# The second half of a down tile one pair later in its group of eight pairs

## The chip, the cores and the metric

The kernel runs on 1 core of one Trainium2 chip. The metric is the device time in microseconds of one execution: 1829.32 us in the median of 3 runs (1829.18 to 1830.04).

## The reference

One transformer block, prompt phase, in float32: adaptive layer norm, full attention with 32 heads of 16, and a SwiGLU feed-forward network. S = 2048 rows, D = 512, F = 1792.

```python
mod = (_silu(c) @ w_mod).reshape(c.shape[0], 6, 1, -1)      # sa, ca, ga, sb, cb, gb
h = _layernorm(x) * (1 + ca) + sa
q, k, v = split(h @ wqkv)                                    # 32 heads of 16
p = softmax(q @ k.T * 16 ** -0.5)
x = x + ga * ((p @ v) @ wo)
h = _layernorm(x) * (1 + cb) + sb
x = x + gb * ((_silu(h @ w_gate) * (h @ w_up)) @ w_down)
```

## The kernel before, in words

A float32 product is made of three products of rounded parts: every large operand is held as a high and a low part, and high x high, high x low and low x high are added up in one PSUM bank. For the scores the parts of a head stand below each other, so that one matmul over 48 or 50 rows does all of it.

**Pairs.** Attention is cut into units, one for each of four column chunks of 512 queries and each of eight groups of four heads, and each unit into 16 steps of 128 keys. One step has four **pairs** (`pair_of`, lines 977 to 989). A pair is one score matmul (`score`, line 563: keys x queries of one head into a bank, and behind it, on ACT, the exp of line 571 which reads that bank and writes a tile `pt_`) and one matmul for the row maxima of a later unit (`max_one`, line 512, with the reduce of line 523 on DVE). The two stand in opposite halves of the 128 rows, so TensorE runs them side by side. Pairs with an even head put the score first, the others the maximum. The maxima run ahead of the scores by LEAD steps, so in the last 80 pairs there are none.

**PV.** `pv_step` (line 573) multiplies the exps with the values, half a step at a time, four matmuls side by side; it follows the scores at a distance (line 1017).

**Filler.** Beside attention the feed-forward network of the chunk before is worked off: the jobs of line 695 in a list, `gate_up` (line 842) and `down` (line 866). A job is a generator (`accumulate`, line 776) which issues one step of two matmuls for each `take`. The matmuls are again over half the rows each: in the first half of the job the tile `outs[0]` is fed from rows 0 to 63 and `outs[1]` from rows 64 to 127 side by side, in the second half they trade rows. A gate/up job has 48 steps; it is spread over two groups. A down job has 12 steps, 6 for each half, and lies in one group. The two tiles are banks 3 and 6 (FBANKS).

**The trade of a down tile.** Before the second half of a down job may add into the banks from the other rows, `read_both` (line 891) has ACT copy one element of each bank (line 893); the second half's matmuls wait for these copies. A gate/up job has no such copies. Behind the last step of a down job DVE adds both banks to the residual rows (line 870), and with t0 = 2 the load of the next down weights is issued on SP's queue (line 880).

**Groups.** `filled` (line 1056) issues one group: eight pairs, and behind pair r as many steps of the job as `places[r]` says; then what `hook` holds back, then six PV half-steps, then `turns_behind`. Calls that are due at a step come behind pairs 3 and 7. In a group the scores use banks 4 and 5 in turn and the maxima banks 0, 1 and 2 (line 1060). Once the maxima are over, the row of places is looked up in `ALONE` and the scores have five banks (line 1062). Groups of gate/up take the row `TWO` twice, each down job takes the row `DOWN` once (line 1103). A down job comes with t0 = 0 and right behind it with t0 = 2. Between the parts of the network there are stretches of pairs without filler (`plain`, line 1041). The order on each engine is the order in which this program issues the instructions.

Of the kernel before, what the change touches and what calls it, by code (L numbers as in the profile page):

```python
# [47 lines left out]
NORM = 9  # L48
STARTS = (147, 275, 403)
TWO = (0, 3, 2, 2, 2, 2, 1, 0)  # L50
DOWN = (0, 3, 3, 0, 3, 3, 0, 0)
ALONE = {TWO: (0, 4, 0, 4, 0, 4, 0, 0), DOWN: (0, 6, 0, 0, 0, 6, 0, 0)}


# [47 lines left out]
def block_kernel(ctx, tc, x, wqkv, wo, w_gate, w_up, w_down, c, w_mod, out):  # L102
# [953 lines left out]
    def filled(places, work):  # L1056

        nonlocal four, bank, beside
        beside = True
        four, bank = three, Turn(4, 5)  # L1060
        if done >= 4 * n - 4 * (LEAD - 1):
            places, bank = ALONE.get(places, places), Turn(4, 5, 0, 1, 2)
        for r in range(len(places)):
            pair_of()
            take(work, places[r])
            if r % 4 == 3:
                end_steps()
        hook()
        pvs(6, False)
        turns_behind()  # L1070
# [14 lines left out]
    for ci in range(last):  # L1085
# [12 lines left out]
        for _ in range(len(ch.jobs) - (KEEP if ci == last - 1 else 0)):  # L1098
# [3 lines left out]
            work = job(ch, *args, outs, True)  # L1102
            for places in (TWO, TWO) if job is gate_up else (DOWN,):
                filled(places, work)
# [80 lines left out]
```

## Time and profile before

| | |
|---|---|
| median of 3 runs | 1829.32 us (1829.18 to 1830.04) |
| span of the profiled execution, first to last instruction | 1827.6 us |
| granted TensorE clock, mean | 1.000 |
| down tiles beside attention | 38 |

The profile gives a span for the profiled execution and no time of its own beside it; the 1.7 us between the span and the median of the runs lie before the first and behind the last instruction. PE stands for TensorE's matmuls and PEld for its weight loads, DVE for VectorE, ACT for ScalarE, POOL for GpSimd, SP for SyncE, whose queue issues DMAs. L569 is line 569 of the kernel. In a timeline row stand the start and the duration in us, engine, line, operation, tiles written and read, and in brackets how long the engine sat idle before it and what ended that. A duration of several merged instructions (x6) reaches from the first start to the last end. A matmul's duration is longer than its slot: the next matmul starts before its end.

### The profile page before, as it was taken

To read this page: it belongs to the slowest core of one execution; us is meant where nothing else is said; L and a number is where in the kernel's file an instruction comes from. 1 tells how busy PE (TensorE), PEld (TensorE's weight loads), DVE (VectorE), ACT (ScalarE), POOL (GpSimd) and SP (SyncE) were. 2 spreads that over 40 slices of the span, in tenths; PEclk is the share of its full clock that TensorE was granted. 3 is DMA by queue.
4 is the path that set the end of the run, shared out by engine and by line. 5 is a ranking of instruction groups with operands and counts; after the bars stand their busy time and mean duration, and the time that the engine had idled before them with its cause. 6 is when DMAs were issued, how large, how long until landed. Compare 5 with 4: busy or idle time off the path is not lost.

```text
span 1827.6 us, 41072 instructions
## 1 busy us (share of the span) xinstructions
PE 1818.3 (99%) x16904; PEld 1199.7 (66%) x16904; DVE 1523.2 (83%) x2554; ACT 1255.7 (69%) x2434; POOL 459.9 (25%) x538
## 2 busy tenths in 40 slices
PE   9999999999999999999999999999999999999999
PEld 7876444444455777776565777776464577767887
DVE  5578999999999888889999888889999988821544
ACT  4223888888888776777888777777888877774211
POOL 3612544556223111111123111111113011130200
PEclk9999999999999999999999999999999999999999
DMA  9884876667845454453544554444643536333742
GB/s 306 288 225 143 202 195 178 178 167 200 206 81 125 103 123 142 114 148 71 144 110 107 139 125 119 124 115 91 160 79 57 119 89 162 130 119 120 276 167 110
DMA packets 80488, 267.63 MB, mean 146 GB/s; under 512 B 19604, under 2 KB 24212, under 8 KB 59620
## 3 DMA queue, kind: packets, MB, share of 16 engines
q1 hardware_dynamic: 61324, 179.71, 34.1%
q0 software_dynamic: 18288, 84.49, 19.4%
q8 instruction: 133, 2.18, 0.5%
q10 hardware_dynamic: 688, 0.80, 0.2%
q14 instruction: 55, 0.45, 0.1%
HBM read 201.85 MB, written 62.13 MB: 144 GB/s over the span
## 4 chain that ended last, share of the span: by engine, by line
PE 82%; DVE 14%; ACT 1%; DMA 1%; issue 0%; SPq 0%; DVEq 0%; ACTq 0%
PE bank L584 21%; PE bank L786 20%; PE bank L569 14%; DVE mx L523 14%; PE bank L521 11%; PE bank L211 7%; PE bank L796 7%; DMA wm_ab<-in_w_mod 1%; PE bank L770 0%; DMA kop<-o_dr 0%; PE bank L163 0%; DMA rb<-d_dr 0%; ACT sq L820 0%; PE bank L839 0%; DVE v_flat L870 0%
## 5 line engine op out<-in xcount | busy, mean ns | idle before, releaser
L523 DVE TENSOR_REDUCE mx<-bank 128x1 f32<-128x512 f32 x2048 | 1274.3, 686 | 108.3 <-PE bank L521 54.6
L569 PE MATMUL bank<-qop,kop 50*128 50x512 f32 x2048 | 728.6, 425 | 0.4 <-ACT pt__16523 L571 0.2
L521 PE MATMUL bank<-kop,qop 48*128 48x512 f32 x2048 | 725.1, 425 | 0.3
L569 PEld LDWEIGHTS bank<-qop,kop 50*128 50x128 f32 x2048 | 343.6, 184 | 167.9 <-issue 49.7
L521 PEld LDWEIGHTS bank<-kop,qop 48*128 48x128 f32 x2048 | 344.0, 185 | 107.0 <-DVE mx L523 62.3
L786 PE MATMUL bank<-act,wgu 64*128 64x512 f32 x1872 | 301.4, 392 | 0.0
L786 PEld LDWEIGHTS bank<-act,wgu 64*128 64x128 f32 x1872 | 197.1, 187 | 24.3
L611 POOL TENSOR_TENSOR on<-o,rb 128x512 f32<-128x512 f32 x31 | 39.8, 1285 | 506.3 <-DMA rb<-d_dr 358.9
L786 PE MATMUL bank<-wd,mid 64*128 64x512 f32 x912 | 134.1, 397 | 0.1
L858 POOL CAST mid<-m 128x512 fp32r<-128x512 f32 x40 | 24.3, 607 | 380.9 <-DVE m L856 180.2
L786 PEld LDWEIGHTS bank<-wd,mid 64*128 64x128 f32 x912 | 88.3, 186 | 15.5 <-ACT first L893 3.2
L211 PE MATMUL bank<-hT,wqs 128*128 128x512 f32 x384 | 94.4, 397 | 0.4 <-DVE wqs L351 0.4
L854 DVE SCALAR_TENSOR_TENSOR q<-th,bank 128x512 f32<-128x512 f32 x56 | 38.2, 683 | 54.3 <-ACT th L850 54.3
L211 PEld LDWEIGHTS bank<-hT,wqs 128*128 128x128 f32 x384 | 70.7, 188 | 18.8 <-issue 2.9
L850 ACT ACTIVATE th<-bank 128x512 f32<-128x512 f32 x56 | 33.3, 594 | 57.9 <-PE bank L796 57.9
L870 DVE TENSOR_TENSOR x<-bank,x 128x512 f32<-128x512 f32 x84 | 53.9, 685 | 19.0 <-PE bank L786 16.8
L856 DVE TENSOR_TENSOR m<-bank,q 128x512 f32<-128x512 f32 x56 | 38.7, 692 | 21.7 <-PE bank L796 19.7
L859 POOL TENSOR_TENSOR mid<-m,mid 128x512 fp32r<-128x512 f32 x40 | 51.6, 1289 | 3.3
L796 PE MATMUL bank<-wd,mid 128*128 128x512 f32 x216 | 51.5, 394 | 0.0
L211 PE MATMUL bank<-wqs,hT 128*128 128x512 f32 x192 | 48.1, 398 | 0.0
L786 PE MATMUL bank<-wgu,act 64*128 64x512 f32 x288 | 47.0, 393 | 0.0
L796 PEld LDWEIGHTS bank<-wd,mid 128*128 128x128 f32 x216 | 40.4, 188 | 9.0 <-POOL mid L859 0.2
(6301 smaller groups left out, 5148.9 us busy)
## 6 DMA issues: line engine op xcount, KB each, us to landing
wgu<-gu_dr SPq DMA_DIRECT2D x48, 1024.0 KB
wd<-wd_dr SPq DMA_DIRECT2D x28, 1024.0 KB
kop<-kd SPq DMA_DIRECT2D x33, 768.0 KB
kop<-kd POOLq DMA_DIRECT2D x29, 768.0 KB, 8.7
gu_dr<-wgu POOLq DMA_DIRECT2D x14, 1024.0 KB, 13.6
kd<-prt SPq DMA_DIRECT2D x16, 512.0 KB
qd<-prt SPq DMA_DIRECT2D x16, 512.0 KB
kop<-gu_dr SPq DMA_DIRECT2D x8, 1024.0 KB
```

The source lines that it names most:

```text
L211: nc.tensor.matmul(pt, lhs(a, k), rhs(b, k), start=(n == 0), stop=(n == 3 * nk - 1))
L521: nc.tensor.matmul(pm, qop[u][rows, s, qt * P:(qt + 1) * P], kop[u % 3][rows, s, kc * CW:(kc + 1) * CW], start=True, stop=True)
L523: nc.vector.tensor_reduce(mx[u][:, b, s, qt, kc:kc + 1], pm, op=ALU.max, axis=AX.X)
L569: nc.tensor.matmul(sp, kop[u % 3][rows, h // 2, kt * P:(kt + 1) * P], qop[u][rows, h // 2, :], start=True, stop=True)
L584: nc.tensor.matmul(pv[u][32 * h:32 * h + 32, cols], v_flat[:, e0:e0 + 32], p_[h][:, cols], start=(kt == 0 and half == 0), stop=(kt == 15), ...
L611: mul.tensor_mul(on, o, rb)
L786: nc.tensor.matmul(outs[e], lhs(e, a, k)[rows], rhs(b, k)[rows], start=(ph == 0 and j == 0), stop=(j == z and (ph == 1 or trade is not None)),
L796: nc.tensor.matmul(outs[e], lhs(e, a, k), rhs(b, k), start=(j == 0), stop=(j == z))
L854: nc.vector.scalar_tensor_tensor(q, th, 1.0, outs[0], op0=ALU.add, op1=ALU.mult)
L856: nc.vector.tensor_mul(m32, outs[1], q)
L859: (nc.gpsimd if slow else nc.vector).tensor_sub(mid[:, 1, :], m32, mid[:, 0, :].bitcast(F32))
L870: nc.vector.tensor_add(ch.x2[:, t, :], outs[e], ch.x2[:, t, :])
```

## The change

The row of places of a down job that lies beside attention is another one. The six steps of the first half stay behind pairs 1 and 2 (pairs are counted from 0); the six of the second half stand behind pairs 5 and 6, not 4 and 5. Between the halves, and so between the copies of line 893 and the matmuls that wait for them, stand pairs 3, 4 and 5, where there were 3 and 4; behind the tile stands pair 7, where there were 6 and 7. `DOWN` as a key of `ALONE` changes with it, its row there stays.

```diff
 TWO = (0, 3, 2, 2, 2, 2, 1, 0)
-DOWN = (0, 3, 3, 0, 3, 3, 0, 0)
+DOWN = (0, 3, 3, 0, 0, 3, 3, 0)
 ALONE = {TWO: (0, 4, 0, 4, 0, 4, 0, 0), DOWN: (0, 6, 0, 0, 0, 6, 0, 0)}
```

## The prediction

> **What bounds the kernel now.** I read the page first, for the chain that ended last, and then the waits of the edited place.
>
> ```profile
> span 1827.6 us, 41072 instructions
> PE 1818.3 (99%) x16904; PEld 1199.7 (66%) x16904; DVE 1523.2 (83%) x2554; ACT 1255.7 (69%) x2434; POOL 459.9 (25%) x538
> PE 82%; DVE 14%; ACT 1%; DMA 1%; issue 0%; SPq 0%; DVEq 0%; ACTq 0%
> ```
>
> PE carries 82% of the chain and DVE 14%. The span is 1827.6 us and the median of the runs 1829.32, so 1.7 us lie around the span; I work in the span and add the 1.7.
>
> Next come the down tile's own rows. The first fence is line 893 (the tiny copies that read both banks between the halves), the second line 870 (the two adds that close a tile) up to the time at which the last row maximum of line 523 is over.
>
> ```profile
> L893 ACT COPY first<-bank x76: 143/148/150, 630.6 to 1658.5; 1x1 f32<-1x1 f32 x76
> who waited for it (us, times):
>   PEld bank L786: 3.2, 16
> ```
> ```profile
> L870 DVE TENSOR_TENSOR x<-bank,x x68: 678/687/693, 632.8 to 1588.2; 128x512 f32<-128x512 f32 x68
> ```
>
> Two copies and two adds belong to each tile. So 76/2 = 38 down tiles stand beside attention, and 68/2 = 34 of them while row maxima still run; the other 4 take the row that the table ALONE gives for them, which the diff leaves as it is. All that PE waits for the copies is 3.2 us in 16 waits. This 3.2 us bounds what covering the trade better can win directly.
>
> The third view is the table of stretches. The first sum is over the 17 groups of tiles with t0 = 0, each from its first pair to the next group's first pair, the second over the 17 with t0 = 2. The last two rows are one gate/up group with the same 8 pairs, 12 filler steps and 6 PV steps, and the longest down group.
>
> ```profile
> sum 116.25, PE 116.25 PEld 83.25 DVE 108.66 ACT 79.91 POOL 39.88; mean PE 6.84 PEld 4.90 DVE 6.39 ACT 4.70 POOL 2.35
> ...
> sum 117.81, PE 117.69 PEld 82.66 DVE 109.12 ACT 81.67 POOL 8.09; mean PE 6.92 PEld 4.86 DVE 6.42 ACT 4.80 POOL 0.48
> ...
> 641.90:648.65 6.75, 6.75 (x78) 4.95 (x74) 5.55 (x10) 4.56 (x8) 0.00 (x0) 1.00 0.68 279
> ...
> 716.47:723.67 7.20, 7.08 (x76) 4.80 (x73) 6.58 (x13) 4.63 (x10) 0.00 (x0) 1.00 0.14 20
> ```
>
> A down group takes 6.84 or 6.93 us, against 6.75 for the same slots in a gate/up group. The present place of the second half thus costs 0.09 to 0.18 us a group, 116.25 + 117.81 - 34 x 6.75 = 4.6 us in all. DVE is busy for 6.4 of the 6.9 us, ACT for 4.7: PE is the bound, DVE is close behind.
>
> The last view is the timeline of the first group (t0 = 0), and of the places in the second (t0 = 2) where it differs. I count the pairs of a group from 0.
>
> ```profile
> 628.18 0.18 PEld L569 LDWEIGHTS bank<-qop,kop 50*128 50x128 f32 x1 [0.41 <-issue]
> 628.74 0.87 PE L786 MATMUL bank<-wd,mid 64*128 64x512 f32 x6
> 629.43 0.39 PE L521 MATMUL bank<-kop,qop 48*128 48x512 f32 x1
> 629.45 0.41 PE L569 MATMUL bank<-qop,kop 50*128 50x512 f32 x1
> 629.67 0.89 PE L786 MATMUL bank<-wd,mid 64*128 64x512 f32 x6
> 629.90 0.60 ACT L571 ACTIVATE pt__7336<-bank 128x512 f32<-128x512 f32 x1
> 630.37 0.39 PE L521 MATMUL bank<-kop,qop 48*128 48x512 f32 x1
> 630.40 0.64 PE L569 MATMUL bank<-qop,kop 50*128 50x512 f32 x2
> 630.55 0.18 PEld L569 LDWEIGHTS bank<-qop,kop 50*128 50x128 f32 x1 [0.19 <-ACT pt__7336 L571]
> 630.55 0.18 PEld L521 LDWEIGHTS bank<-kop,qop 48*128 48x128 f32 x1
> 630.56 0.20 ACT L893 COPY first<-bank 1x1 f32<-1x1 f32 x2
> 630.63 0.42 PE L521 MATMUL bank<-kop,qop 48*128 48x512 f32 x1
> 630.83 0.60 ACT L571 ACTIVATE pt__7349<-bank 128x512 f32<-128x512 f32 x1
> 630.88 0.90 PE L786 MATMUL bank<-wd,mid 64*128 64x512 f32 x6
> 631.32 0.59 ACT L571 ACTIVATE pt__7352<-bank 128x512 f32<-128x512 f32 x1
> 631.62 0.39 PE L569 MATMUL bank<-qop,kop 50*128 50x512 f32 x1
> 631.85 0.86 PE L786 MATMUL bank<-wd,mid 64*128 64x512 f32 x6
> 632.82 1.29 DVE L870 TENSOR_TENSOR x<-bank,x 128x512 f32<-128x512 f32 x2
> 633.12 0.11 PEld L584 LDWEIGHTS bank<-pt__7263,v_flat 128*32 128x32 f32 x1 [0.24 <-issue]
> 634.02 1.28 DVE L523 TENSOR_REDUCE mx<-bank 128x1 f32<-128x512 f32 x2
> 634.98 0.18 PEld L569 LDWEIGHTS bank<-qop,kop 50*128 50x128 f32 x1 [0.41 <-issue]
> ...
> 637.64 0.60 ACT L571 ACTIVATE pt__7433<-bank 128x512 f32<-128x512 f32 x1
> 637.71 0.54 PEld L786 LDWEIGHTS bank<-wd,mid 64*128 64x128 f32 x6 [0.16 <-ACT first L893]
> 640.03 0.11 PEld L584 LDWEIGHTS bank<-pt__7352,v_flat 128*32 128x32 f32 x1 [0.25 <-issue]
> ```
>
> Pair 2 is at 629.43, then the three steps that end the first half, pair 3 at 630.37, pair 4 at about 630.6, the second half from 630.88, pair 5 inside it at 631.62, the rest of it from 631.85, pairs 6 and 7, and PV from 633.12. A slot of PE (a pair, or a step of two matmuls) is about 0.23 us: 631.62 to 631.85. What matters most is the row at 630.55. The scores have two banks in turn, 4 and 5, so pair 4 needs the bank that the exp of pair 2 (pt__7336) reads until 630.50; its weight load starts 0.05 us later, its matmuls at 630.63. From score to free bank a bank is thus away for 630.55 - 629.45 = 1.1 us. Two pairs in a row with three steps ahead of them just fit into that, since PE comes to pair 4 at 630.37 + 0.23 = 630.60 anyhow.
>
> **The change part by part.** 34 groups change. The number of instructions on PE, ACT, DVE and every queue stays; only places move.
>
> The copies. They stand behind pair 2 as before and PE now comes to the second half a pair later. They are done by 630.56 + 0.20 = 630.76, so the waits on them end in the 34 groups. That is the gain aimed at, at most 0.18 us in a group.
>
> The third pair. Pair 5 now follows pair 4 directly. It takes the bank of pair 3, whose exp (pt__7349) stands behind the copies on ACT, starts at 630.83 and ends at 631.43. PE is ready for pair 5 at 630.63 + 0.23 = 630.86. With the release that pair 4 shows (630.50 to 630.63, of which I take 0.11) pair 5 starts at 631.54: PE stands for 0.68 us. Behind the waiting score in PE's queue stand the maximum of pair 5 and all twelve matmuls of the second half; behind those wait DVE's adds and the maxima, and nobody else's work fills the hole. The second half then starts 0.25 us later, at 631.79 (630.63 to 630.88 is that step after the held pair 4). From there to PV stood 633.12 - 630.88 = 2.24 us with three pairs in it; one pair fewer makes 2.01. PV starts at 633.80, 0.68 us later than before.
>
> For t0 = 2 the same sum starts from the exp at 637.64: it ends at 638.24, pair 5 starts at 638.35, the second half at 638.60, PV at 640.61 against 640.03, so 0.58 us later. Here the wait on the copies and its aftermath (the 0.09 us by which these groups are longer) is what is won.
>
> A rule of matmul order bears on this. Both weight loads at 630.55 start together, the one of the maximum in the other half of the rows too: nothing passed the held score there. The Trainium skill, "TensorE: Matmul & The Clock Gate", Part 3, says that matmuls start and end in program order while weight loads may be pulled ahead of running ones; by the first half of it the hold reaches all that follows, by the second the restart would be hidden, 0.02 us less a group or 0.7 us in all (no row here shows a load passing a held one).
>
> The adds. They come after the maximum of pair 6 instead of pair 5. The second half runs from 631.79 over three steps to pair 6 at 632.48 and over three more from 632.71; the adds started 0.97 us behind the first of the last three (631.85 to 632.82), so now at 633.68, 0.86 us later, and end at 634.97 after their 1.29. The next group starts at 634.98 + 0.68 = 635.66, and its first step into banks 3 and 6 comes behind its pair 1, 0.56 us on (628.18 to 628.74 in this group), at 636.22: 1.25 us to spare, cost nothing. The cover is that spare time; beyond it each us of delay counts in full.
>
> The DMAs. The load of the next down weights is issued behind the last step with t0 = 2, about 0.9 us later, and the gate/up load behind it on SP's queue moves with it. In the emitted order nothing on SP or POOL changes places, since a group's other calls come behind pairs 3 and 7. The gate/up load of 640.05 is read one group pair later, two times 6.75 us, and the wait table shows no wait of PE for it; I take nothing.
>
> ```profile
> 640.05 0.42 SPq L715 DMA_DIRECT2D wgu<-gu_dr  x1
> ```
>
> Sum: 17 x 0.68 + 17 x 0.58 = 21.4 us. Bounds: if pair 5 starts as the exp ends and the restart is one bare slot, t0 = 2 gives 638.24 + 0.23 + 2.01 - 640.03 = 0.45 us, and 34 x 0.45 = 15.3; if every held restart drags as the second half after 637.71 does (0.09 more), 0.77 x 34 = 26.2. Nothing below zero comes out unless pair 5 is not held at all, which is a rival.
>
> **The rivals.** Forecast: held third pair, 1827.6 + 21.4 + 1.7 = 1850.7 us, range 1844.6 to 1855.5.
>
> Not held: pair 5 finds its bank free when PE comes, since ACT has slack (4.7 of 6.9 us busy). Then the groups come down to the 6.75 of the gate/up group, -4.6 us, 1824.7. It decides at the exp of pair 3: that would have to end by 630.75 and not at 631.43. For it speaks only ACT's mean load; against it, that its score starts no earlier than 630.37 and none of the exps shown takes under 0.59. Were it that matmuls behind the held score pass it, the time would be about the same, 1824.7.
>
> DVE falls behind: reduces and adds, 6.4 us in a group of 7.5, come in a clump after the hold and the adds end over 1.25 us late, so that the next tile waits. The worst group on the page, 7.20 against 6.93, gives a price of 0.3: 10 us more, 1860.9. Against it: the hold gives DVE more time, not more work.
>
> That the diff would not act where it should is no case: the key of ALONE is the same name as the row.
>
> **How the numbers follow.** Held 0.86, not held 0.08, DVE behind 0.06. A measurement of this kernel tells about 0.2%, 3.7 us, from no change. Held and DVE behind are slower, 0.92; not held is split between the full 4.6 us and less, faster 0.04 and same 0.04. The range 1844 to 1856 is that of the held case and leaves out 0.14.
>
> **What would show it.** In the changed profile: the weight load of pair 5's score idle about 0.7 us in each of the 34 groups, ended by the exp of pair 3; down groups of 7.5 us for both t0, gate/up groups still 6.75; waits on line 893 down to the four tiles without maxima; the adds behind three reduces and no wait of line 786 on them. Wrong would be a third score that starts before that exp's end, or groups longer than 7.6 us, which would point to DVE.

## The result and the profile after

The changed kernel takes 1848.87 us (1848.37 to 1850.34) against 1829.25 us before: 19.6 us more, a ratio of 1.011 with a 95% interval of 1.0097 to 1.0123. The span of its profiled execution is 1846.7 us, 19.1 more than before.

First the page of the changed kernel: span, and the chain by engine.

```profile
span 1846.7 us, 41083 instructions
PE 82%; DVE 14%; ACT 3%; issue 1%; DMA 0%; SPq 0%; DVEq 0%; ACTq 0%
```

PE's share stays at 82%, ACT's goes from 1% to 3%: at some places the chain now runs over ACT. The table of stretches says where the time is. The first sum is over the 17 groups with t0 = 0, the second over those with t0 = 2, and the last row is the gate/up group that follows the first two.

```profile
sum 127.47, PE 120.40 PEld 81.03 DVE 116.07 ACT 81.73 POOL 39.67; mean PE 7.08 PEld 4.77 DVE 6.83 ACT 4.81 POOL 2.33
...
sum 127.57, PE 120.10 PEld 80.26 DVE 110.75 ACT 83.52 POOL 7.84; mean PE 7.06 PEld 4.72 DVE 6.51 ACT 4.91 POOL 0.46
...
642.11:648.86 6.75, 6.75 (x76) 5.02 (x72) 5.22 (x9) 4.57 (x8) 0.00 (x0) 1.00 0.69 285
```

Both kinds of down group now take 7.50 us, 127.47 - 116.25 = 11.2 and 127.57 - 117.81 = 9.8 us more, 21.0 in all; the gate/up group keeps its 6.75. (A gate/up job has 24 steps, 12 in each of its two groups, not 48: `TWO` adds up to 12.) PE's busy time is on average 0.42 us short of the stretch in a group with t0 = 0 (127.47 - 120.40 over 17), where it filled the stretch before. The hole is seen in the timeline of the first group.

```profile
627.16 0.18 PEld L569 LDWEIGHTS bank<-qop,kop 50*128 50x128 f32 x1 [0.41 <-issue]
...
629.35 0.39 PE L521 MATMUL bank<-kop,qop 48*128 48x512 f32 x1
629.39 0.63 PE L569 MATMUL bank<-qop,kop 50*128 50x512 f32 x2
629.53 0.18 PEld L569 LDWEIGHTS bank<-qop,kop 50*128 50x128 f32 x1 [0.18 <-ACT pt__7336 L571]
629.55 0.20 ACT L893 COPY first<-bank 1x1 f32<-1x1 f32 x2
629.63 0.41 PE L521 MATMUL bank<-kop,qop 48*128 48x512 f32 x1
629.83 0.60 ACT L571 ACTIVATE pt__7349<-bank 128x512 f32<-128x512 f32 x1
630.32 0.59 ACT L571 ACTIVATE pt__7352<-bank 128x512 f32<-128x512 f32 x1
630.47 0.18 PEld L569 LDWEIGHTS bank<-qop,kop 50*128 50x128 f32 x1 [0.76 <-ACT pt__7349 L571]
630.47 0.50 PE L569 MATMUL bank<-qop,kop 50*128 50x512 f32 x1 [0.44 <-ACT pt__7349 L571]
630.81 0.87 PE L786 MATMUL bank<-wd,mid 64*128 64x512 f32 x6
631.95 0.69 DVE L523 TENSOR_REDUCE mx<-bank 128x1 f32<-128x512 f32 x1 [0.21 <-PE bank L521]
632.73 1.29 DVE L870 TENSOR_TENSOR x<-bank,x 128x512 f32<-128x512 f32 x2
632.77 0.11 PEld L584 LDWEIGHTS bank<-pt__7263,v_flat 128*32 128x32 f32 x1 [0.37 <-issue]
633.93 0.68 DVE L523 TENSOR_REDUCE mx<-bank 128x1 f32<-128x512 f32 x1
634.64 0.18 PEld L569 LDWEIGHTS bank<-qop,kop 50*128 50x128 f32 x1 [0.41 <-issue]
```

Up to 629.63, pair 4, this is the group of before, 1.0 us earlier. Then pair 5's score waits for pt__7349, the exp of pair 3, which ends at 629.83 + 0.60 = 630.43, and starts at 630.47. I call such a wait a hold. Two numbers in these rows tell of it and neither is its length. The weight loads sat idle for 0.76 us, but PE was still at work for part of it. The matmuls sat idle for 0.44, but that counts only from the end of the matmul before, whose tail normally overlaps the next. The length is the start against the start without a hold: 630.47 - (629.63 + 0.23) = 0.61 us. The other down groups show the same: without a hold pair 5's score would start 0.23 us behind pair 4's, and in the 34 groups it starts 0.88 to 0.94 us behind it, once 1.07.

The second view is line 893 of the changed kernel.

```profile
who waited for it (us, times):
  PEld bank L786: 1.1, 4
```

From 16 waits and 3.2 us, 4 waits and 1.1 us are left, those of the four tiles without maxima. The change does what it says: the trade is covered in all 34 groups. What covers it is longer than the wait was.

### The profile page after: what moved, and what is told of

It reads as the page before. It is cut to its first block, busy times and chain, and to the rows that moved or that the text cites. A ratio compares the mean times of both kernels' runs of the same rounds, so it can differ in the third digit from the quotient of the medians.

```text
span 1846.7 us, 41083 instructions
## 1 busy us (share of the span) xinstructions
PE 1823.2 (99%) x16904; PEld 1192.9 (65%) x16904; DVE 1525.5 (83%) x2554; ACT 1259.3 (68%) x2434; POOL 459.7 (25%) x538
## 3 DMA queue, kind: packets, MB, share of 16 engines
q0 software_dynamic: 18288, 84.49, 19.1%
## 4 chain that ended last, share of the span: by engine, by line
PE 82%; DVE 14%; ACT 3%; issue 1%; DMA 0%; SPq 0%; DVEq 0%; ACTq 0%
PE bank L584 21%; PE bank L786 19%; PE bank L569 14%; DVE mx L523 14%; PE bank L521 10%; PE bank L796 8%; PE bank L211 7%; PE bank L839 1%; PE bank L770 0%; DMA wm_ab<-in_w_mod 0%; PE bank L163 0%; ACT sq L820 0%; DVE v_flat L870 0%; PE bank L535 0%; ACT first L893 0%
## 5 line engine op out<-in xcount | busy, mean ns | idle before, releaser
L569 PE MATMUL bank<-qop,kop 50*128 50x512 f32 x2048 | 736.3, 427 | 14.9 <-ACT pt__8512 L571 0.6
L521 PE MATMUL bank<-kop,qop 48*128 48x512 f32 x2048 | 733.3, 426 | 0.3
```

Source lines behind the costliest of these rows:

```text
L521: nc.tensor.matmul(pm, qop[u][rows, s, qt * P:(qt + 1) * P], kop[u % 3][rows, s, kc * CW:(kc + 1) * CW], start=True, stop=True)
L569: nc.tensor.matmul(sp, kop[u % 3][rows, h // 2, kt * P:(kt + 1) * P], qop[u][rows, h // 2, :], start=True, stop=True)
```

## The experiments

My theory is the round trip: a score bank is away for about 1.1 us from its score to the end of its exp, there are two, and so the third score in a row waits. The rivals are that the two copies ahead of the exp on ACT cause the delay, that DVE's pace does (6.4 us of work in the group), and that the later place of the second half costs by itself. For each kernel the fence shows the sum over its 34 down groups from the table of stretches (before: 234.06, or 6.88 a group; changed: 255.04, or 7.50), and, where the verdict rests on them, rows of the timeline. The first four ran beside the kernel before at 1829.34 us.

**Four pairs in a row.**

```diff
-DOWN = (0, 3, 3, 0, 0, 3, 3, 0)
+DOWN = (0, 3, 3, 0, 0, 0, 3, 3)
```

> The second half behind pairs 6 and 7, four pairs in a row before it. Round trip (my theory: the third score in a row waits until the exp of two pairs earlier has left its bank): pair 5 is held until 3.3 us from the group's first pair as in the changed kernel, pair 6 in turn until the exp of pair 4 ends, about 3.8; the second half starts at 4.1, a group takes 7.73 us and the kernel 1857 us. Rival, copies: the two copies ahead of the exp of pair 3 cause the hold once; a further pair adds nothing, 7.50 us and 1849. Rival, DVE: the maxima of the pairs in a row run out of their three banks and DVE's 0.65 us a reduce is the pace; four pairs add one reduce, 8.1 us and 1870.

```profile
sum 263.51, PE 248.99 PEld 164.60 DVE 223.20 ACT 161.58 POOL 47.00; mean PE 7.32 PEld 4.84 DVE 6.56 ACT 4.75 POOL 1.38
```
```profile
630.49 0.18 PEld L569 LDWEIGHTS bank<-qop,kop 50*128 50x128 f32 x1 [0.76 <-ACT pt__7349 L571]
630.98 0.18 PEld L569 LDWEIGHTS bank<-qop,kop 50*128 50x128 f32 x1 [0.19 <-ACT pt__7352 L571]
```

1856.73 us, 7.75 us a group. The fourth score waits in its turn for the exp of pair 4, 0.49 us behind the third, which is the distance of two exps on ACT (629.83 and 630.32 above). That speaks for the round trip; DVE's 8.1 us a group and the copies' single hold are out as the pace here.

**One step between pairs 4 and 5, and two.**

```diff
-DOWN = (0, 3, 3, 0, 0, 3, 3, 0)
+DOWN = (0, 3, 3, 0, 1, 2, 3, 0)
```
```diff
-DOWN = (0, 3, 3, 0, 0, 3, 3, 0)
+DOWN = (0, 3, 3, 0, 2, 1, 3, 0)
```

> One step of the second half behind pair 4, two behind pair 5, three behind pair 6. Round trip: pair 5 still starts at 3.3 us, but 0.25 us of the hold is filled with the step; group 7.25 us, kernel 1840.5 us. Rival, copies: the step waits for the copies, and nothing of the hold is filled, 7.50 and 1849. Rival, DVE: the pace of three reduces is the same, 7.50 and 1849.

> Two steps of the second half behind pair 4, one behind pair 5, three behind pair 6. Round trip: pair 5 comes due at 3.17 us and is held until 3.3; group 6.98 us, 0.1 above the kernel before, kernel 1832 us. Rival, place: if each slot by which the second half starts later has its own price, one step in three is left, 7.09 us and 1835. Rivals copies and DVE: as for one step, 7.50 and 1849.

```profile
sum 246.90, PE 242.64 PEld 161.05 DVE 225.13 ACT 165.22 POOL 47.54; mean PE 7.14 PEld 4.74 DVE 6.62 ACT 4.86 POOL 1.40
```
```profile
630.37 0.18 PEld L569 LDWEIGHTS bank<-qop,kop 50*128 50x128 f32 x1 [0.48 <-ACT pt__7349 L571]
```
```profile
sum 239.47, PE 239.34 PEld 161.24 DVE 220.85 ACT 162.02 POOL 47.21; mean PE 7.04 PEld 4.74 DVE 6.50 ACT 4.77 POOL 1.39
```
```profile
631.00 0.18 PEld L569 LDWEIGHTS bank<-qop,kop 50*128 50x128 f32 x1 [0.36 <-ACT pt__7349 L571]
```

1840.43 us and 7.26 a group with one step, 1833.25 us (ratio 1.0018, interval 1.0009 to 1.0028) and 7.04 with two. So the price goes 7.50, 7.26, 7.04, 6.88 with none, one, two and three steps between. The copies and DVE, by which nothing would be won, are out as causes of the whole. But the steps are nearly even, and 7.04 lies midway between the 6.98 of the round trip and the 7.09 of the place (the rival by which the later place costs by itself): the times of these two runs don't tell those theories apart. The rows speak for the round trip. In both runs pair 5 still waits for the exp of pair 3 and starts 3.30 us into its group (the groups start at 627.07 and 627.70), and with two steps it was due at 3.18.

**A spare bank.** The score of pair 5 in down groups takes a bank of the maxima's ring; the maximum of pair 5 is held over and issued ahead of pair 6. `lone` is true at pair 5 of a down group, and `r` is the number of the maximum. A bank that is handed to `score` is used in place of the one in turn.

```diff
...
+        r = done + 4 * (LEAD - 1)
         work = [lambda: score(i + 1, h)]
-        if done < most:
-            work.insert(1 - h % 2, lambda: max_one(done + 4 * (LEAD - 1)))
+        if lone and done < most:
+            held.append(r)
+            spare = four("spare")
+            work = [lambda: score(i + 1, h, spare)]
+        elif done < most:
+            work.insert(1 - h % 2, lambda: max_one(r))
+            if held:
+                work.insert(0, lambda: max_one(held.pop()))
...
```

> The changed kernel, but the score of pair 5 in down groups goes to a bank of the maxima's ring, which the maximum of pair 2 has left by then; the maximum of pair 5 is issued with pair 6, so a group has one slot of PE more. Round trip: no hold at pair 5, which starts at 2.65 us; group 6.75 + 0.23 = 6.98 us, kernel 1831.5 us. Rival, copies: the bank does not matter, 7.5 to 7.7 us, 1849 to 1857. Rival, DVE: the same reduces in the same order, 7.5 us and 1849.

```profile
sum 247.09, PE 243.56 PEld 166.46 DVE 225.00 ACT 161.76 POOL 47.64; mean PE 7.16 PEld 4.90 DVE 6.62 ACT 4.76 POOL 1.40
```
```profile
629.41 0.41 PE L521 MATMUL bank<-kop,qop 48*128 48x512 f32 x1
629.66 0.39 PE L569 MATMUL bank<-qop,kop 50*128 50x512 f32 x1
629.67 1.09 PE L786 MATMUL bank<-wd,mid 64*128 64x512 f32 x6
630.41 1.01 PE L521 MATMUL bank<-kop,qop 48*128 48x512 f32 x2
630.92 0.18 PEld L521 LDWEIGHTS bank<-kop,qop 48*128 48x128 f32 x1 [0.42 <-DVE mx L523]
```

1841.96 us, 7.27 a group: less than half of the gain that I expected (7.50 to 6.98). The hold at pair 5 is gone (its score starts 0.25 us behind pair 4, at 629.66, and the second half beside it). In its place the maximum of pair 6 waits for a reduce, since the ring of three banks had lent one. The weight loads sit idle for 0.42 us there; the maximum itself starts 0.28 us late, at 630.92 and not at 630.41 + 0.23. My number missed this wait, and the slot more that I had counted is not there.

The next three ran beside the kernel before at 1828.74 us.

**The same, without the spare bank.** The control moves the maximum in the same way, but the score of pair 5 takes its bank in turn.

```diff
             held.append(r)
             spare = four("spare")
-            work = [lambda: score(i + 1, h, spare)]
+            work = [lambda: score(i + 1, h, None)]
```

> The counterpart of the run with the spare bank: the maximum of pair 5 is issued with pair 6 as there and the maxima's ring skips a bank as there, but the score of pair 5 takes its bank in turn, that of pair 3. Round trip: pair 5 is held until 3.3 us again, the hold at pair 6 goes since DVE has had time; group 7.4 to 7.5 us, kernel 1846 to 1849 us. Rival, DVE: what was won with the spare bank came from moving the maximum, so it is won here too, 7.2 us or less and 1842 or less.

```profile
sum 255.60, PE 241.00 PEld 162.15 DVE 218.67 ACT 165.33 POOL 47.08; mean PE 7.09 PEld 4.77 DVE 6.43 ACT 4.86 POOL 1.38
```
```profile
629.81 0.18 PEld L569 LDWEIGHTS bank<-qop,kop 50*128 50x128 f32 x1 [0.73 <-ACT pt__7349 L571]
```

1849.96 us, 7.52 a group, and the old hold for the exp of pair 3. Place, copies and the moved maximum are the same in these two kernels. What differs is the bank of pair 5's score, and with it which of banks 4 and 5 the later scores take: it is the bank. This settles what the times with one and two steps left open; the place of the second half has no price of its own that these runs show.

**The copies behind the exp of pair 3.** `read_both` is called behind pair 3 instead of with the last step of the first half.

```diff
-                          halves and read_both)
+                          halves and (lambda: trades.append(read_both)))
...
             pair_of()
+            if r == 3:
+                while trades:
+                    trades.pop()()
```

> The changed kernel with the two copies of the trade issued behind pair 3, so on ACT behind the exp of pair 3 instead of ahead of it. Round trip: that exp starts 0.45 us after its score with or without the copies, 2.66 us from the group's first pair; pair 5 still starts at 3.3, group 7.5 us, kernel 1849 us. Rival, copies: the 0.2 us of the copies stand in the exp's way; pair 5 starts at 3.1, group 7.3, kernel 1842 us.

```profile
sum 254.62, PE 240.40 PEld 161.48 DVE 226.75 ACT 160.93 POOL 47.65; mean PE 7.07 PEld 4.75 DVE 6.67 ACT 4.73 POOL 1.40
```
```profile
630.05 0.65 PE L569 MATMUL bank<-qop,kop 50*128 50x512 f32 x2
630.48 0.60 ACT L571 ACTIVATE pt__7347<-bank 128x512 f32<-128x512 f32 x1 [0.33 <-PE bank L569]
630.98 0.18 ACT L893 COPY first<-bank 1x1 f32<-1x1 f32 x2
631.13 0.18 PEld L569 LDWEIGHTS bank<-qop,kop 50*128 50x128 f32 x1 [0.74 <-ACT first L893]
```

1849.19 us, 7.49 a group. The exp of pair 3 starts 0.43 us behind its score, 0.44 in the changed kernel (629.39 to 629.83): it waits for its score and not for the copies. The last row is a reading to beware of. It names a copy as what ended the wait, since one ended close by; the exp ended at 631.08, 0.05 us ahead of the load, about the distance of the other holds (0.04 in the changed kernel). The copies are out.

**Swapped banks.** The spare bank as above, and the score bank that is left over goes to the held maximum, so that the ring isn't a bank short.

```diff
...
-            held.append(r)
+            held.append((r, bank("held")))
...
-                work.insert(0, lambda: max_one(held.pop()))
+                work.insert(0, lambda: max_one(*held.pop()))
...
```

> As with the spare bank, but the bank that the score of pair 5 leaves free is given to the maximum of pair 5, issued with pair 6: the two trade banks, and the maxima's ring is not a bank short. Round trip, with the hold at pair 6 in the spare-bank run read as a want of a maxima bank: neither hold is left, the score of pair 5 and the maximum run in opposite row halves beside steps, so no slot is added; group 6.75 to 6.85 us, kernel 1826 to 1829 us, as fast as the kernel before or up to 0.2% faster. Rival, DVE: the pair 6 hold is DVE's pace, not a bank; it stays, 7.2 us and 1842.

```profile
sum 240.06, PE 240.06 PEld 168.46 DVE 220.78 ACT 161.59 POOL 47.47; mean PE 7.06 PEld 4.95 DVE 6.49 ACT 4.75 POOL 1.40
```
```profile
630.48 0.43 PE L786 MATMUL bank<-wd,mid 64*128 64x512 f32 x1
630.48 0.38 PE L569 MATMUL bank<-qop,kop 50*128 50x512 f32 x1
630.71 0.85 PE L786 MATMUL bank<-wd,mid 64*128 64x512 f32 x5
631.22 0.58 PE L521 MATMUL bank<-kop,qop 48*128 48x512 f32 x2
631.55 0.18 PEld L569 LDWEIGHTS bank<-qop,kop 50*128 50x128 f32 x1 [0.21 <-ACT pt__7352 L571]
```

1833.92 us (ratio 1.0033, interval 1.0020 to 1.0046), 7.06 a group. Both holds are gone, as expected, but a third is there: pair 6 comes so early now that its own bank, that of pair 4, isn't back. My 6.75 to 6.85 was wrong for the reason that the theory names.

**The kernel before again**, for its trace.

> The kernel before once more, for its trace. The groups of the changed kernel account for 21.0 us and its span is 19.1 us longer; 1.0 of the missing 1.9 us lies ahead of the first down group. If that is from one execution to the next, the first down group starts up to 1 us from 628.18 here, and the down groups' sum is 234.1 within 0.3. If it belongs to the change, it starts at 628.2 again.

```profile
sum 234.17, PE 234.04 PEld 165.28 DVE 217.83 ACT 161.65 POOL 48.05; mean PE 6.88 PEld 4.86 DVE 6.41 ACT 4.75 POOL 1.41
```
```profile
627.49 0.18 PEld L569 LDWEIGHTS bank<-qop,kop 50*128 50x128 f32 x1 [0.41 <-issue]
```

Its span is 1826.1 us, and its first down group starts at 627.49, 0.7 us earlier than in the first trace of the same kernel, while the groups' sum differs by 0.1. So the stretch ahead of the first down tile differs by some tenths from one execution to the next, and the groups' 21.0 us are the better measure of the change than the spans' 19.1 (20.6 against this trace).

**Four and five steps behind pair 5**, with the swapped banks, beside the kernel before at 1829.66 us. If only pair 6 came later, no bank should be late.

```diff
-DOWN = (0, 3, 3, 0, 0, 3, 3, 0)
+DOWN = (0, 3, 3, 0, 0, 4, 2, 0)
```
```diff
-DOWN = (0, 3, 3, 0, 0, 3, 3, 0)
+DOWN = (0, 3, 3, 0, 0, 5, 1, 0)
```

> The swapped banks with four steps behind pair 5 and two behind pair 6. In the run with swapped banks pair 6 was held, from 3.45 us when PE came to its maxima until the exp of pair 4 had left bank 4 at about 3.75. Round trip: one step more ahead of it brings PE there at about 3.9, and no score is held; group 6.80 us, kernel 1826 us, 0.15% faster than the kernel before. Rival, slots: the loose score and maximum of pair 5 cost a slot of PE whatever the banks do; group 7.0 us, kernel 1833 us.

> The swapped banks with five steps behind pair 5 and one behind pair 6. Round trip: pair 6 comes later still, no hold there; but pair 7 follows it after one step, and its bank is the one of the moved maximum, whose reduce DVE ends about 4.6 us: held for 0.0 to 0.2 us; group 6.8 to 7.0 us, kernel 1826 to 1833 us. Rival, slots: 7.0 us and 1833.

```profile
sum 245.54, PE 245.54 PEld 175.94 DVE 221.17 ACT 161.57 POOL 47.39; mean PE 7.22 PEld 5.17 DVE 6.50 ACT 4.75 POOL 1.39
```
```profile
633.92 0.18 PEld L569 LDWEIGHTS bank<-qop,kop 50*128 50x128 f32 x1 [0.33 <-DVE mx L523]
```
```profile
sum 253.03, PE 247.25 PEld 176.00 DVE 221.22 ACT 161.53 POOL 47.39; mean PE 7.27 PEld 5.18 DVE 6.51 ACT 4.75 POOL 1.39
```

1839.51 us and 7.22 a group, 1848.87 us and 7.44: both worse than three steps, against what I expected of either. Pair 6 isn't held any more, but pair 7's score needs the bank that was given to the held maximum, whose reduce comes the later, the later pair 6 is (0.33 us of idle with four steps). For five steps I had named this wait but put it at 0.2 us at most, which was too little; for four I had missed it. The slots' 7.0 us is wrong too: the time is a hold again, at another bank.

No version found here beats the kernel before. A trade that needs no copies might win part of the 4.6 us of the prediction at the old places; that wasn't tried, since the order of the halves in a bank rests on the copies.

## Why the prediction was right

**The trade.** At most 0.18 us a group was to be won, and the waits on line 893 were to end. In the 34 groups they did; the two kinds of group, 0.09 us apart before, are the same now.

**The third pair.** Pair 5 was to start 631.54 - 628.18 = 3.36 us into the group; it starts at 630.47 - 627.16 = 3.31. The release was shorter than the 0.11 us that I took from pair 4: 0.04, from the exp's end to load and matmul at once. That it is the bank, and neither the copies nor DVE, was argued there and is shown by the spare bank, its control and the moved copies.

**The restart** was mis-sized the other way: the second half begins 0.34 us behind the held score (630.47 to 630.81), not 0.25. The row that I took it from was itself a hold, of a smaller kind: at pair 4 the loads waited but the matmuls ahead still ran. The row to take stood in the kernel before at the first pair of the same group, where load and matmul also start together, at 628.18, and the next pair comes 0.34 us later:

```profile
628.18 0.49 PE L569 MATMUL bank<-qop,kop 50*128 50x512 f32 x1
628.52 0.38 PE L569 MATMUL bank<-qop,kop 50*128 50x512 f32 x1
```

Here I had also said what the Trainium skill, "TensorE: Matmul & The Clock Gate", Part 3, would make of it: loads may be pulled ahead of running matmuls, so the restart could be hidden. In this trace the held score's load and matmul start together at 630.47 and nothing behind them was loaded before, so at this hold the first half of that rule, matmuls in program order, agrees, and the second buys nothing. The first half does not agree everywhere. In the run with swapped banks one step matmul starts at 630.48, beside the score of pair 5, and the next at 630.71; the kernel issues the matmul in the score's own rows first, so the one at 630.48, in the other half, has passed it.

**The sum.** 0.68 and 0.58 us a group were predicted, 0.66 and 0.57 measured (11.22 and 9.76 over 17). In the first group three errors cancel: the held score is 0.05 us earlier than I had it, the restart 0.09 longer, and from the second half to PV it takes 632.77 - 630.81 = 1.96 us and not 2.01. So the mechanism and the size of the hold were right, and that the sum comes this close is in part luck. 21.4 us predicted, 21.0 in the groups, 19.6 in the runs (17.7 to 22.5 by the interval); the rest lies outside the groups, at least part of it ahead of the first, where two traces of the one unchanged kernel differ by 0.7 us.

**The adds** start at 632.73, 5.57 us into the group (5.50 predicted), and end 0.6 us ahead of the next group: nobody waits for them, and the rival of DVE falling behind didn't come. PE did wait for DVE, for a reduce and not for the adds, where an experiment took a bank from the maxima. **The DMAs** cost nothing that the groups show, as I had it.

The rival that pair 5 isn't held failed at the point named for it: the exp of pair 3 would have had to end by 2.57 us into the group (630.75 against 628.18) and ends at 3.27. Nor did matmuls behind the held score pass it: the steps start at 630.81.

## What to carry to other kernels

Work that covers a wait must not need anything that the wait's neighbours hold: count, for each kind of cover, the buffers that it takes and the time until one is back. Here a run of n pairs needs n free score banks or 1.1 us for every two, and a busy share of two thirds on ACT says nothing of that. Where all banks are taken, a bank lent to one place is missing at another: four kernels each ended one hold and met the next.

## What the runs showed of the hardware

- A score and a maximum that were taken apart took no slot of PE more than a pair. In the spare-bank run the loose score starts at 629.66 and a step matmul at 629.67; the six step matmuls take 1.09 us where they took 0.87 in the changed kernel, one slot more, and the loose maximum starts at 630.41, before they end at 630.76. In that run the halves are still not independent: the score of pair 6 starts with the held maximum of the other half, at 630.92, though its own bank was back at 630.21. So a matmul that waits for a bank kept back both halves there, while one that only waited for its own half (630.48 and 630.71 in the run with swapped banks) did not.
- A matmul released from a hold delays what follows it by 0.34 us instead of 0.23, and shows 0.50 us of duration instead of 0.39. So does the first pair of a group, which was not held (0.34 and 0.49): at both, load and matmul start together.
- Two copies of one element each, ahead of an exp on ACT, didn't delay it, since its score took as long: 0.44 us from score to exp with the copies ahead, 0.43 without.
